# Attention and mixture of experts on one core: ScalarE copies the 16-bit planes, and a fifth expert's tokens are turned by DMA

## The chip, the core and the metric

The kernel runs as one program on one of the eight cores of a Trainium2 chip. The metric is the device time of one execution in microseconds (us); lower is better. Five engines work side by side, each on its own queue of instructions in a fixed order: TensorE (PE, matrix products), VectorE (DVE), ScalarE (ACT), GpSimd (POOL) and SyncE (SP, which here only issues DMA transfers). An instruction that waits holds up everything that stands behind it in its engine's queue.

## The reference, cut to what matters

```python
# attention: 8 batches, 8 heads, 576 positions, width 64, window of 128, a bias by distance
scores = scale * q @ k.T + bias;  attn = softmax(scores, masked);  x = (attn @ v)   # x: 4608 tokens x 512
# mixture of experts: 8 experts, each takes exactly cap = 4608 / 8 = 576 tokens
logits = x @ w_gate
for idx in argsort(-logits.flatten()):          # greedy: best pair first, until an expert is full
    ...
for e in range(8):
    h = maximum(x[assigned == e] @ w1[e], 0)    # 576x512 @ 512x1024
    out[assigned == e] = h @ w2[e]              # 576x1024 @ 1024x512
```

All of it is float32. Which tokens an expert gets is known only when the router has run, and an expert's list depends on which experts are already full.

## The kernel before, in words

**Attention** takes the first 230 us or so and is not touched. It leaves the tokens x in DRAM, one row of 512 floats for each token.

**The experts** follow one after another. "Expert k" below is the k-th in the order of processing, counted from 0, so the fourth expert is expert 3. Each float32 factor is split into a high and a low part (names ending in h and l), and a product is the sum of three matmuls. Layer 1 of an expert (`layer1`, L1041) runs over 8 blocks f of 128 hidden units; a block is 24 matmuls into two PSUM banks of a ring of four (`ph`). ScalarE then applies the ReLU into `hh` (L1064) and VectorE computes the low part `hlo` (L1069). Layer 2 (`layer2`, L1073) runs over five tiles t of tokens, 24 matmuls for each of the first four (L1087, L1088, L1090) and 16 for the last, into a ring of two banks (`po`); ScalarE copies a tile out (L1094) and GpSimd scatters it to DRAM (L1099). ScalarE and VectorE also split the weights, chunk by chunk (`split`, L965 and L967), after SyncE has loaded them (L958).

**The tokens of the next expert** are fetched by GpSimd with five indirect DMAs (`gather`, L976), one for each 128 tokens (the last has 64). A matmul needs them with features on the partitions, so each tile must be turned. There are two ways:

- `turn` (L987): PE transposes each tile in four pieces into one PSUM bank `pg` (L1000), ScalarE rounds it into `xh` (L1003), VectorE takes the rest into `xl` (L1004). All five tiles share that one bank. Experts 0 to 3 are turned in this way.
- `turn_by_dma` (L1008): the 32-bit words are taken apart into two planes of 16 bits (`pl`, two copies on GpSimd for each tile, L1017), SyncE issues a transposing DMA for each tile (`tp`, L1022), and two more copies on GpSimd join the planes to words again (`xf`, L1029). ScalarE and VectorE then make `xh` and `xl` (L1037, L1038). Experts 4 to 7 are turned in this way. All of `g`, `pl`, `tp` and `xf` live in one ring of seven buffers.

**The router** (`Router.phase`) runs in between, in small steps: for each next expert, several rounds of counting, each a VectorE indicator (L586), eight small matmuls (L610), a VectorE comparison and one more small matmul (L630); then sums (L760, L786, L787), the one-hot tables `loOH` and `mv` on VectorE (L812, L808, L809), 18 small matmuls that give the list (L817), and `idx` (L825). These small matmuls stand in PE's queue between those of the layers.

**What sets the order.** `layer_moe` calls `slot(k, i)` after each half block and each third of a tile, i counting from 0 to 30 within expert k. A slot advances the router when its count of slots to wait (table `WAITS`) has run out, loads and splits a chunk of weights, and takes the next step of the turning. `DMA_AT` holds, step by step, the slot from which a step of `turn_by_dma` may be taken: one step for the gathers, then five each for `pl`, `tp`, `xf` and `xh`/`xl`. `BY_DMA = 3` starts that way in the slots of expert 3, that is with the tokens of expert 4. The calls only give an order of creation; a scheduler then orders each engine's queue by its own estimates. A dependency marked `BEHIND` is seen by that scheduler alone and adds no wait on the chip; the transposes already have one ("weights first").

Of the kernel before, what the change touches and what calls it, by code (L numbers as in the profile page):

```python
# [423 lines left out]
TURN0 = 3  # L424
BY_DMA = 3
DMA_AT = [0, 1, 1, 2, 2, 2, 7, 7, 7, 7, 7, 9, 9, 10, 10, 10, 17, 19, 21, 23, 25]
BEHIND = mybir.DependencyInfo(mybir.DependencyClass.NoSync, mybir.DependencyReason.SCHED_ONLY)
# [32 lines left out]
class Router:  # L460
# [255 lines left out]
    def phase(self, k, exact=False):  # L716
# [94 lines left out]
        for a, z in ((0, 18), (18, 30), (30, NT)) if k == 0 else ((0, NT),):  # L811
            nc.vector.tensor_tensor(loOH[:, a:z], bc(self.C["i64"].rearrange("p (s o) -> p s o", o=2).unsqueeze(1), [128, z - a, 32, 2]),  # L812
                                    bc(slo[:, a:z].unsqueeze(2), [128, z - a, 32, 2]), ALU.is_equal)
        yield WAITS[6] + (k < 4)
        ip = self.bank()
# [13 lines left out]
        if k < 7:  # L829
            self.pen = self.small("pen", 8)  # L830
            nc.vector.tensor_scalar(self.pen, Dc, float(CAP), -BIG, ALU.is_ge, ALU.mult)
            self.base = self.small("base", 8)
            nc.vector.tensor_tensor(self.base, self.pen, Dc, ALU.add)
            nc.vector.scalar_tensor_tensor(self.left, keyv, mx[:, 0:1], self.left, ALU.not_equal, ALU.mult)
            L2 = rt.tile([128, 8, NT], F32, name="L2", bufs=1)
            eng = nc.vector if k == 0 or k > BY_DMA else self.tc.nc.gpsimd
            eng.tensor_tensor(L2, L, bc(self.pen.unsqueeze(2), [128, 8, NT]), ALU.add)
            if k == 0 or k > BY_DMA:
                nc.vector.scalar_tensor_tensor(self.L1, T1, 100.0 * BIG, L2, ALU.mult, ALU.add)
            else:  # L840
# [106 lines left out]
class MoE:  # L947
# [39 lines left out]
    def turn(self, gs, first=False):  # L987
# [6 lines left out]
        for h, (g, r) in enumerate(gs):  # L994
# [11 lines left out]
            yield  # L1006

    def turn_by_dma(self, idx, asked):  # L1008

# [3 lines left out]
        for g, r in gs:  # L1013
            pl = ring.tile([128, 2, DM], U16, name="pl", tag="g")
            words = g.bitcast(U16).rearrange("q (c o) -> q c o", o=2)
            for a in range(2):
                nc.gpsimd.tensor_copy(pl[:r, a, :], words[:r, :, 1 - a])  # L1017
            pls.append((pl, r))
            yield
        for pl, r in pls:  # L1020
# [3 lines left out]
            yield  # L1024
        for tp, r in tps:
            xf = ring.tile([128, 4, 128], F32, name="xf", tag="g")
            words = xf.rearrange("q j t -> q (j t)").bitcast(U16).rearrange("q (j t o) -> q j t o", j=4, o=2)
            for a in range(2):
                nc.gpsimd.tensor_copy(words[:, :, :r, 1 - a], tp[:, 4 * a:4 * a + 4, :r])  # L1029
            xfs.append((xf, r))  # L1030
            yield
        xh = self.p["xg"].tile([128, 4, CAP], F32R, name="xh")
        xl = self.p["xg"].tile([128, 4, CAP], F32R, name="xl")
        self.xg = xh, xl
        for h, (xf, r) in enumerate(xfs):
            o = slice(128 * h, 128 * h + r)
# [4 lines left out]
    def layer1(self, w1, xg, first=False):  # L1041
# [7 lines left out]
        for f, ts in order:  # L1049
# [12 lines left out]
            for t in ts:  # L1062
                o = hh[:, f, cut[t]:cut[t + 1]]
                nc.scalar.activation(o, pp[t], AF.Relu)  # L1064
                e = min(512, cut[t + 1])
# [7 lines left out]
    def layer2(self, w2, h, idx, last=False):  # L1073
        nc = self.nc
        hh, hl = h
        for t in range(5) if not last else (4, 0, 1, 2, 3):
# [4 lines left out]
            for cs in cols:  # L1081
# [11 lines left out]
                if t < 4:  # L1093
                    nc.scalar.copy(o[:, cs], po[:, cs])  # L1094
                else:
# [55 lines left out]
def layer_moe(tc, P, C, r, x, w1, w2, out, exact):  # L1151
# [29 lines left out]
    def slot(k, i):  # L1181
# [23 lines left out]
        if k >= BY_DMA and k + 1 in r.idx:  # L1205
            if k not in gathers:
                asked[k + 1] = []
                gathers[k], st["made"] = m.turn_by_dma(r.idx[k + 1], asked[k + 1]), 0
            while st["made"] < len(DMA_AT) and i >= DMA_AT[st["made"]]:
                next(gathers[k])  # L1210
                st["made"] += 1
# [106 lines left out]
```

## Time and profile before

| | |
|---|---|
| median of three runs | 692.59 us (692.06 to 695.39) |
| the profiled execution | 690.85 us, span of its instructions 688.9 us |
| expert 2, layer 1 and layer 2 | 356.64 to 385.30, 385.30 to 415.99 us of the span |
| expert 3 | 415.99 to 443.80, 443.80 to 471.17 |
| expert 4 | 471.17 to 498.25, 498.25 to 526.54 |
| expert 5 | 526.54 to 553.11, 553.11 to 579.48 |
| expert 6 | 579.48 to 605.06, 605.06 to 630.47 |

Each stage begins with the first matmul of its layer on PE's timeline. All times inside the span are counted from its start. In a list of waits, the engine, line and tile that waited stand left of the arrow, and what ended the wait on its right.

### The profile page before, as it was taken

Reading aid. Unit: us, or ns where it says so; the run is one execution under the profiler, and the core shown is the slowest. Engines: PE = TensorE matmul, PEld = TensorE weight load, DVE = VectorE, ACT = ScalarE, POOL = GpSimd, SP = SyncE. Lnnn points to the kernel's source line nnn. Section 1 sums busy time; section 2 is a strip of 40 time slices with the busy share of each in tenths; the row PEclk is TensorE's granted clock in tenths of the full one; section 3 lists DMA queues with packets and bytes.
Section 4 is the critical chain, followed back from the end, with each engine's and each line's share of the span. In section 5 each row is a group of like instructions: output and inputs, shape, how many; then the busy total and the mean of one; then the engine's idle time right before and its main releaser. Section 6 shows DMA issues by size and latency. Waiting matters only on the chain.

```text
span 688.9 us, 18916 instructions
## 1 busy us (share of the span) xinstructions
PE 657.4 (95%) x7171; PEld 582.2 (85%) x7172; DVE 479.1 (70%) x1985; ACT 332.1 (48%) x991; POOL 192.7 (28%) x376
## 2 busy tenths in 40 slices
PE   7999999999995699999999999999989999999995
PEld 4898998998985399889789779979978978988985
DVE  5788888888887899879669788886775734532310
ACT  6898888888884262334134224324323333432210
POOL 4021221211220301511422017255076075152011
PEclk9999999999997799999999999999999999999998
DMA  8456566566532453615417227635625644621001
GB/s 307 148 181 202 175 193 200 166 211 186 161 106 70 124 191 104 241 39 187 158 36 245 88 92 245 131 106 182 133 98 166 167 111 169 160 52 54 1 25 49
DMA packets 54212, 97.47 MB, mean 141 GB/s; under 512 B 22880, under 2 KB 32224, under 8 KB 54112
## 3 DMA queue, kind: packets, MB, share of 16 engines
q1 hardware_dynamic: 48224, 77.30, 37.0%
q0 software_dynamic: 5888, 18.88, 8.3%
q8 instruction: 58, 0.95, 0.6%
q14 instruction: 42, 0.34, 0.1%
HBM read 72.57 MB, written 18.87 MB: 133 GB/s over the span
## 4 chain that ended last, share of the span: by engine, by line
PE 77%; DVE 12%; DMA 6%; issue 2%; ACT 1%; SPq 1%; POOL 0%; POOLq 0%; DVEq 0%; ACTq 0%
PE ph L1059 20%; PE po L1087 9%; PE po L1088 9%; PE s L54 8%; PE pt L54 7%; PE pt L158 7%; PE po L1090 7%; PE x L54 6%; DMA raw<-in_w_dram 2%; DVE hl L967 2%; DMA tp<-pl 1%; DVE hlo L1069 1%; DMA craw<-in_cst_dram 1%; PE pg L1000 1%; DMA qk<-in_qk_dram 1%
## 5 line engine op out<-in xcount | busy, mean ns | idle before, releaser
L1059 PE MATMUL ph<-xh,hl 128*128 128x288 f32 (+2 forms) x1024 | 188.9, 299 | 0.7 <-DVE lo L534 0.5
L1059 PEld LDWEIGHTS ph<-xh,hl 128*128 128x128 f32 x1024 | 154.7, 189 | 2.4 <-ACT hh L1064 1.0
L145 ACT ACTIVATE u<-u,mn 128x192 f32<-128x192 f32 (+2 forms) x288 | 123.9, 433 | 24.6 <-DVE mn L134 24.5
L1087 PE MATMUL po<-hl,hh 128*128 128x512 f32 (+1 forms) x328 | 128.9, 393 | 0.6 <-ACT o L1094 0.6
L1088 PE MATMUL po<-hl,hh 128*128 128x512 f32 (+1 forms) x328 | 126.4, 385 | 0.0
L967 DVE TENSOR_TENSOR hl<-raw,hl 128x512 fp32r<-128x512 f32 x128 | 88.1, 708 | 48.6 <-ACT hl L965 48.1
L1059 PE MATMUL ph<-xl,hl 128*128 128x288 f32 (+2 forms) x512 | 115.1, 297 | 0.0
L1064 ACT ACTIVATE hh<-ph 128x288 fp32r<-128x288 f32 (+2 forms) x128 | 46.6, 408 | 131.9 <-PE ph L1059 128.8
L134 DVE CUSTOM_DVE_ANT_0 u<-s,bm 128x192 f32<-128x192 f32 x308 | 86.5, 333 | 29.8 <-PE s L54 29.2
L1090 PE MATMUL po<-hl,hlo 128*128 128x512 f32 (+1 forms) x264 | 101.3, 384 | 0.0
L1099 POOL DMA_INDIRECT out_dram<-o,idx x40 | 42.5, 1063 | 153.1 <-ACT o L1094 76.0
L1059 PEld LDWEIGHTS ph<-xl,hl 128*128 128x128 f32 x512 | 84.1, 189 | 0.0
L965 ACT CAST hl<-raw 128x1024 fp32r<-128x1024 f32 x64 | 65.8, 1050 | 25.1 <-DMA raw<-in_w_dram 22.0
L1069 DVE SCALAR_TENSOR_TENSOR hlo<-ph,hh 128x288 fp32r<-128x288 f32 (+2 forms) x128 | 49.4, 417 | 35.8 <-ACT hh L1064 35.1
L1087 PEld LDWEIGHTS po<-hl,hh 128*128 128x128 f32 x328 | 61.8, 188 | 12.3 <-ACT o L1094 1.0
L54 PE MATMUL s<-qk 64*64 64x192 f32 (+1 forms) x1112 | 69.6, 319 | 2.5 <-DVE mn L134 1.8
L1088 PEld LDWEIGHTS po<-hl,hh 128*128 128x128 f32 x328 | 61.8, 188 | 11.0
L1094 ACT COPY o<-po 128x512 f32<-128x512 f32 (+1 forms) x33 | 18.8, 572 | 95.7 <-PE po L1090 77.4
L976 POOL DMA_INDIRECT g<-x,idx x40 | 42.1, 1053 | 72.2 <-issue 31.7
L1090 PEld LDWEIGHTS po<-hl,hlo 128*128 128x128 f32 x264 | 49.6, 188 | 10.0
L158 PE MATMUL pt<-ident_sb,u 128*128 128x128 f32 x368 | 54.2, 282 | 1.4 <-DVE mn L134 1.0
L54 PEld LDWEIGHTS s<-qk 64*64 64x64 f32 x1112 | 48.3, 132 | 8.3 <-issue 2.2
(240 smaller groups left out, 925.8 us busy)
## 6 DMA issues: line engine op xcount, KB each, us to landing
raw<-in_w_dram SPq DMA_DIRECT2D x64, 512.0 KB, 4.4
qk<-in_qk_dram SPq DMA_DIRECT2D x32, 576.0 KB, 4.8
v<-in_v_dram SPq DMA_DIRECT2D x32, 288.0 KB, 3.8
x<-xb SPq DMA_DIRECT2D x14, 512.0 KB, 3.5
x<-xb SPq DMA_DIRECT2D x8, 128.0 KB, 3.3
x<-xb SPq DMA_DIRECT2D x4, 256.0 KB, 2.4
g<-x,idx POOLq DMA_INDIRECT x40, 3.9
out_dram<-o,idx POOLq DMA_INDIRECT x40, 3.2
```

Source lines behind the costliest of these rows:

```text
L54: put(nc.tensor.matmul(out, w, a, start=start, stop=stop, skip_group_check=True))
L134: put(nc.vector.tensor_tensor_reduce(out=u[rows], in0=x[rows, c:c + 64 * m].rearrange("q (j k) -> q j k", k=64), in1=bm[n % NP][rows, y:y ...
L145: put(nc.scalar.activation(u, u, AF.Exp, bias=st["mn"][:, i:i + 1], scale=-1.0, accum_out=st["sm"][:, i:i + 1]))
L158: put(nc.tensor.transpose(ps[:, c:c + 128], u[:, o + 128 * j:o + 128 * j + 128], ident))
L965: self.last = nc.scalar.copy(hl[:, 0, :], raw)
L967: nc.vector.tensor_tensor(hl[:, 1, c:c + 512], raw[:, c:c + 512], hl[:, 0, c:c + 512].bitcast(F32), ALU.subtract)
L1059: nc.tensor.matmul(pp[t], w[:, a, j, fo:fo + 128], x[:, j, cut[t]:cut[t + 1]], start=(i == 0), stop=(i == 11))
L1064: nc.scalar.activation(o, pp[t], AF.Relu)
L1069: nc.vector.scalar_tensor_tensor(d, pp[t][:, c0:c1], 0.0, o[:, c0:c1].bitcast(F32), ALU.max, ALU.subtract)
L1087: nc.tensor.matmul(out, a, wh, start=(f == 0), stop=False)
L1088: nc.tensor.matmul(out, a, wl, start=False, stop=(f == 7 and t == 4))
L1090: nc.tensor.matmul(out, hl[:, f, 128 * t:128 * t + 128], wh, start=False, stop=(f == 7))
```

## The change

Four edits go together.

1. The four plane copies of each tile in `turn_by_dma` move from GpSimd to ScalarE (`nc.scalar.copy`), and each is ordered by the scheduler behind the last ReLU or output copy that ScalarE was given before it (`behind`).
2. Joining a tile and splitting it into `xh` and `xl` become one step instead of two.
3. `BY_DMA` becomes 2: the tokens of expert 3 are turned by DMA as well, and expert 3's PE transposes go.
4. `DMA_AT` becomes a table for expert 2's slots and one for all later ones, and the list of every expert from 4 on is made one slot later (`WAITS[6] + 1` for all).

```diff
-BY_DMA = 3
-DMA_AT = [0, 1, 1, 2, 2, 2, 7, 7, 7, 7, 7, 9, 9, 10, 10, 10, 17, 19, 21, 23, 25]
+BY_DMA = 2
+DMA_AT = {2: [10, 11, 11, 12, 12, 12, 13, 13, 13, 13, 13, 23, 24, 25, 26, 27], 3: [0, 4, 5, 6, 7, 8, 9, 9, 9, 9, 9, 18, 20, 22, 24, 26]}
...
-        yield WAITS[6] + (k < 4)
+        yield WAITS[6] + 1
...
-            eng = nc.vector if k == 0 or k > BY_DMA else self.tc.nc.gpsimd
+            eng = nc.vector if k == 0 or k > 3 else self.tc.nc.gpsimd
...
+    def behind(self, copy):
+        self.tc.add_manual_dep(copy.ins, self.acted.ins.name, BEHIND, reason="layers first")
+
     def turn_by_dma(self, idx, asked):
...
-                nc.gpsimd.tensor_copy(pl[:r, a, :], words[:r, :, 1 - a])
+                self.behind(nc.scalar.copy(pl[:r, a, :], words[:r, :, 1 - a]))
...
-        for tp, r in tps:
+        xh = self.p["xg"].tile([128, 4, CAP], F32R, name="xh")
+        xl = self.p["xg"].tile([128, 4, CAP], F32R, name="xl")
+        self.xg = xh, xl
+        for h, (tp, r) in enumerate(tps):
             xf = ring.tile([128, 4, 128], F32, name="xf", tag="g")
             words = xf.rearrange("q j t -> q (j t)").bitcast(U16).rearrange("q (j t o) -> q j t o", j=4, o=2)
             for a in range(2):
-                nc.gpsimd.tensor_copy(words[:, :, :r, 1 - a], tp[:, 4 * a:4 * a + 4, :r])
-            xfs.append((xf, r))
-            yield
...
-        for h, (xf, r) in enumerate(xfs):
+                self.behind(nc.scalar.copy(words[:, :, :r, 1 - a], tp[:, 4 * a:4 * a + 4, :r]))
...
-                nc.scalar.activation(o, pp[t], AF.Relu)
+                self.acted = nc.scalar.activation(o, pp[t], AF.Relu)
...
-                    nc.scalar.copy(o[:, cs], po[:, cs])
+                    self.acted = nc.scalar.copy(o[:, cs], po[:, cs])
...
-            while st["made"] < len(DMA_AT) and i >= DMA_AT[st["made"]]:
+            due = DMA_AT[min(k, 3)]
+            while st["made"] < len(due) and i >= due[st["made"]]:
```

In the changed kernel the copies of `pl` stand on L1020, the transposes on L1025 and the copies of `xf` on L1035.

How the instructions move is seen at three places. The first is ScalarE's queue in layer 1 of expert 2, from its third and fourth block on (a row with x4 is two blocks of the ReLU). Before:

```order
L1064 ACTIVATE hh<-ph 128x288 x4
L965 CAST hl<-raw 128x1024
L1064 ACTIVATE hh<-ph 128x288 x4
L965 CAST hl<-raw 128x1024
L1064 ACTIVATE hh<-ph 128x288 x4
L965 CAST hl<-raw 128x1024
L1094 COPY o<-po 128x512
L1003 CAST xh<-pg 128x4x128
```

and now:

```order
L1064 ACTIVATE hh<-ph 128x288 x4
L965 CAST hl<-raw 128x1024
L1064 ACTIVATE hh<-ph 128x288 x4
L1020 COPY pl<-g 128x512 x8
L1020 COPY pl<-g 64x512 x2
L1064 ACTIVATE hh<-ph 128x288 x2
L965 CAST hl<-raw 128x1024
L1064 ACTIVATE hh<-ph 128x288 x2
L965 CAST hl<-raw 128x1024
L1094 COPY o<-po 128x512 x2
L1035 COPY xf<-tp 128x512 x2
L1037 CAST xh<-xf 128x4x128
```

All ten `pl` copies of expert 3's tokens stand in one block between the ReLU of block 5 and that of block 6, and a chunk of weights is split after them.

The second place is ScalarE's queue at the end of layer 1 and in layer 2 of expert 3 (the tokens are those of expert 4). Before:

```order
L1064 ACTIVATE hh<-ph 128x288 x4
L1037 CAST xh<-xf 128x4x128 x4
L1037 CAST xh<-xf 128x4x64
L965 CAST hl<-raw 128x1024
L1094 COPY o<-po 128x512 x4
L965 CAST hl<-raw 128x1024 x4
```

and now:

```order
L1064 ACTIVATE hh<-ph 128x288 x4
L965 CAST hl<-raw 128x1024
L1094 COPY o<-po 128x512
L1035 COPY xf<-tp 128x512 x3
L1037 CAST xh<-xf 128x4x128
L1035 COPY xf<-tp 128x512
L1037 CAST xh<-xf 128x4x128
L1094 COPY o<-po 128x512
L1035 COPY xf<-tp 128x512 x2
L1037 CAST xh<-xf 128x4x128
L1094 COPY o<-po 128x512
```

The five `xh` stood ahead of the first output copy; now they follow it, with their `xf` copies, spread between the output copies. The slots of experts 4, 5 and 6 read the same.

The third place is VectorE's queue in layer 2 of expert 4, where the list of expert 6 is made (`hif` to `mv`) and the tokens of expert 5 are split (`xl`). Before:

```order
L1038 TENSOR_TENSOR xl<-xf,xh 128x4x128
L847 SCALAR_TENSOR_TENSOR ov<-kmx,ov 128x1
L792 TENSOR_SCALAR hif<-m 128x36
L848 TENSOR_TENSOR flag<-flag,ov 128x1
L500 TENSOR_TENSOR ne<-L_72,b 128x288
L793 TENSOR_SCALAR hif<-hif 128x36
L1038 TENSOR_TENSOR xl<-xf,xh 128x4x128
L795 SCALAR_TENSOR_TENSOR hv<-hif,m 128x72
L800 SCALAR_TENSOR_TENSOR slo<-hif,m 128x72
L797 TENSOR_TENSOR hOH<-c_h_431,hv 128x360
L812 TENSOR_TENSOR loOH<-c_i_429,slo 128x2304
L808 TENSOR_TENSOR mv<-hOH,c_cc 128x36x10
```

and now:

```order
L795 SCALAR_TENSOR_TENSOR hv<-hif,m 128x72
L800 SCALAR_TENSOR_TENSOR slo<-hif,m 128x72
L797 TENSOR_TENSOR hOH<-c_h_431,hv 128x360
L812 TENSOR_TENSOR loOH<-c_i_429,slo 128x2304
L808 TENSOR_TENSOR mv<-hOH,c_cc 128x36x10
L809 TENSOR_SCALAR mv<-hOH,craw 128x36x10
L504 TENSOR_REDUCE am<-cand 128x36
L505 TENSOR_TENSOR OH<-c_eb,am 128x288
L757 TENSOR_TENSOR T_8654<-OH,sel 128x288
L1038 TENSOR_TENSOR xl<-xf,xh 128x4x128 x2
```

Two `xl` stood ahead of `mv`; now all stand behind it, and two halves of a weight split (L967) stand ahead of it instead, above the rows shown. On PE, the 18 matmuls of that list (L817) stand behind 42 matmuls of layer 2 instead of 33, in the layers of experts 3 and 4 alike.

More of the change, by code (lines that the diff above doesn't have):

```diff
@@ L835, in phase @@
             L2 = rt.tile([128, 8, NT], F32, name="L2", bufs=1)
-            eng = nc.vector if k == 0 or k > BY_DMA else self.tc.nc.gpsimd
+            eng = nc.vector if k == 0 or k > 3 else self.tc.nc.gpsimd
             eng.tensor_tensor(L2, L, bc(self.pen.unsqueeze(2), [128, 8, NT]), ALU.add)
-            if k == 0 or k > BY_DMA:
+            if k == 0 or k > 3:
                 nc.vector.scalar_tensor_tensor(self.L1, T1, 100.0 * BIG, L2, ALU.mult, ALU.add)
@@ L1028, in turn_by_dma @@
             for a in range(2):
-                nc.gpsimd.tensor_copy(words[:, :, :r, 1 - a], tp[:, 4 * a:4 * a + 4, :r])
-            xfs.append((xf, r))
-            yield
-        xh = self.p["xg"].tile([128, 4, CAP], F32R, name="xh")
-        xl = self.p["xg"].tile([128, 4, CAP], F32R, name="xl")
-        self.xg = xh, xl
-        for h, (xf, r) in enumerate(xfs):
+                self.behind(nc.scalar.copy(words[:, :, :r, 1 - a], tp[:, 4 * a:4 * a + 4, :r]))
             o = slice(128 * h, 128 * h + r)
```

## The prediction

> **What bounds the kernel now.** First the engines of the page, then the busy times by stage, from layer 1 of expert 2 to layer 2 of expert 6 (columns: start and end, length, busy time and count of PE, its weight loads, VectorE, ScalarE and GpSimd, granted clock, DMA share, GB/s).
>
> ```profile
> PE 657.4 (95%) x7171; PEld 582.2 (85%) x7172; DVE 479.1 (70%) x1985; ACT 332.1 (48%) x991; POOL 192.7 (28%) x376
> ...
> 356.64:385.30 28.66, 27.25 (x223) 26.50 (x221) 27.01 (x108) 9.80 (x19) 7.48 (x8) 1.00 0.58 194
> 385.30:415.99 30.69, 30.11 (x173) 23.27 (x172) 23.42 (x102) 9.04 (x15) 5.57 (x5) 1.00 0.20 67
> 443.80:471.17 27.37, 26.28 (x134) 21.44 (x133) 20.81 (x69) 9.20 (x15) 19.42 (x26) 1.00 0.31 102
> 498.25:526.54 28.29, 26.34 (x134) 21.45 (x133) 15.13 (x34) 9.31 (x15) 22.51 (x28) 1.00 0.33 104
> 553.11:579.48 26.37, 25.75 (x115) 20.94 (x113) 7.33 (x13) 9.22 (x15) 20.75 (x27) 1.00 0.35 115
> 579.48:605.06 25.58, 25.58 (x193) 25.58 (x192) 14.85 (x35) 9.18 (x19) 2.82 (x3) 1.00 0.71 190
> 605.06:630.47 25.41, 25.41 (x114) 21.03 (x113) 7.43 (x13) 8.80 (x14) 12.05 (x14) 1.00 0.15 48
> ```
>
> PE is the bound: in expert 6 it is busy without a gap, 25.58 us for a layer 1 and 25.41 us for the 112 matmuls of a layer 2, so 25.41/112 = 0.227 us from one to the next. The clock is 1.00 everywhere. Time can only be won where a stage is longer than these two: in layer 2 by 5.28 us for expert 2 and by 1.96, 2.88 and 0.96 us for experts 3, 4 and 5. GpSimd, on the other hand, is busy there for some 20 us without setting anything by itself. Who makes PE wait in experts 3 to 5, from the list of waits of PE between 415.99 and 580 us (total, times, longest):
>
> ```profile
> PE m L817 <- DVE mv L809: 3.0, 2, 1.9
> PE po L1087 <- ACT o L1094: 0.6, 1, 0.6
> ```
>
> Two waits for the router's table `mv` and one for an output copy; the rest of the excess is the router's own small matmuls. What makes `mv` and the copy late stands in the timelines of VectorE and ScalarE (start, length, instruction, idle time before it and what ended it):
>
> ```profile
> 446.19 1.07 DVE L1038 TENSOR_TENSOR xl<-xf,xh 128x512 fp32r<-128x512 f32 x1
> ...
> 452.36 0.30 DVE L809 TENSOR_SCALAR mv<-hOH,craw 128x360 bf16<-128x360 bf16 x1
> ...
> 500.85 0.69 DVE L1038 TENSOR_TENSOR xl<-xf,xh 128x512 fp32r<-128x512 f32 x1 [0.86 <-ACT xh L1037]
> ...
> 507.71 0.30 DVE L809 TENSOR_SCALAR mv<-hOH,craw 128x360 bf16<-128x360 bf16 x1
> ...
> 562.91 0.41 ACT L1037 CAST xh<-xf 128x256 fp32r<-128x256 f32 x1 [1.09 <-POOL xf L1029]
> 563.22 1.04 ACT L965 CAST hl<-raw 128x1024 fp32r<-128x1024 f32 x1
> 564.16 1.06 ACT L1094 COPY o<-po 128x512 f32<-128x512 f32 x2
> ```
>
> All three come from the turned tokens: VectorE takes an `xl` before `mv` and waits with it for ScalarE's `xh`; ScalarE waits for GpSimd's last `xf` until 562.9 us and only then comes to the output copies.
>
> **The change, part by part.** *Expert 3's transposes go.* PE's timeline in layer 2 of expert 2 shows them between the matmuls of the layer; here the second, the fourth and the fifth tile:
>
> ```profile
> 397.74 0.39 PE L1090 MATMUL po<-hl,hlo 128*128 128x512 f32 x1
> 397.97 0.60 PE L1000 MATMUL pg<-ident_sb,g 128*128 128x128 f32 x4
> 398.32 0.48 PE L1087 MATMUL po<-hl,hh 128*128 128x512 f32 x1
> ...
> 406.26 0.39 PE L1090 MATMUL po<-hl,hlo 128*128 128x512 f32 x1
> 407.23 0.66 PE L1000 MATMUL pg<-ident_sb,g 128*128 128x128 f32 x4 [0.58 <-DVE xl L1004]
> 407.64 0.47 PE L1087 MATMUL po<-hl,hh 128*128 128x512 f32 x1
> ...
> 411.51 0.40 PE L1090 MATMUL po<-hl,hlo 128*128 128x512 f32 x1
> 411.84 0.46 PE L1000 MATMUL pg<-ident_sb,g 64*128 64x64 f32 x4
> 412.23 0.50 PE L1087 MATMUL po<-hl,hh 128*128 128x512 f32 x1
> ```
>
> From one layer matmul to the next there are 0.58, 1.38 and 0.72 us where 0.227 would do: 0.35, 1.15 (with a wait for the one bank) and 0.49. With three tiles like the first: 3 x 0.35 + 1.15 + 0.49 = **2.7 us**.
>
> *The waits of experts 3 to 5.* By the order in VectorE's queue, no `xl` stands before `mv` any more, and L817 stands nine matmuls later on PE (9 x 0.227 = 2.0 us), which alone covers the longest wait of 1.9. The output copy of a first tile stands ahead of all `xf` and `xh`. So 3.0 + 0.6 = **3.6 us** go. What is late next is `xl` of the last tile, needed when the next layer 1 begins: in experts 3 to 5 ScalarE has some 3 us of copies left after its third output copy, and 5.5 us of PE work (24 x 0.227) until the fourth.
>
> *What a plane copy costs on ScalarE.* No row has ScalarE on 16-bit words. The nearest:
>
> ```profile
> L1017 POOL COPY pl<-g x40: 600/607/1062, 421.1 to 575.3; 128x512 uint16<-128x512 uint16 x32, 64x512 uint16<-64x512 uint16 x8
> L1029 POOL COPY xf<-tp x40: 464/770/1562, 442.7 to 613.2; 128x512 uint16<-128x512 uint16 x32, 128x256 uint16<-128x256 uint16 x8
> L1037 ACT CAST xh<-xf x20: 404/620/625, 444.5 to 613.7; 128x512 fp32r<-128x512 f32 x16, 128x256 fp32r<-128x256 f32 x4
> L1038 DVE TENSOR_TENSOR xl<-xf,xh x20: 408/687/1165, 446.2 to 614.2; 128x512 fp32r<-128x512 f32 x16, 128x256 fp32r<-128x256 f32 x4
> L965 ACT CAST hl<-raw x64: 1040/1050/1060, 233.3 to 628.9; 128x1024 fp32r<-128x1024 f32 x64
> ```
>
> The rows give minimum, median and maximum in ns. ScalarE takes 620 ns for 512 elements and 1050 for 1024, so it goes by elements; below stands 404 ns (256 elements), above GpSimd's 1562 for the same copy. I take 0.6 us, being nearest to ScalarE's own 512 elements; then 20 copies are 12 us for an expert, on an engine busy for 18 of 51 us. The Trainium skill, ScalarE: Activation LUTs, What ACT_TABLE_LOAD costs, gives 186 ns plus 0.833 ns for each element whatever the type, an estimate of 0.61 us; the two ScalarE medians agree with it, and the sum by it would be the same.
>
> *The block of ten in expert 2.* It stands behind the ReLU of block 5. ScalarE's timeline and GpSimd's gathers of that list (first and last of five, then the time to landing):
>
> ```profile
> 377.67 0.71 ACT L1064 ACTIVATE hh<-ph 128x288 fp32r<-128x288 f32 x2 [3.16 <-PE ph L1059]
> ...
> 380.87 0.71 ACT L1064 ACTIVATE hh<-ph 128x288 fp32r<-128x288 f32 x2 [1.55 <-PE ph L1059]
> 385.37 0.71 ACT L1064 ACTIVATE hh<-ph 128x288 fp32r<-128x288 f32 x2 [3.79 <-PE ph L1059]
> ...
> 372.20 1.00 POOL L976 DMA_INDIRECT g<-x,idx  x1 [10.99 <-issue]
> 377.51 0.91 POOL L976 DMA_INDIRECT g<-x,idx  x1 [0.30 <-issue]
> ...
> DMA to landing us min/median/max: 2.9/3.9/7.8
> ```
>
> The first tile is there at 377 us, the last at about 382.3. Ten copies from 378.4 end at 384.4, so the ReLU of block 6 comes at 384.4 instead of 380.9, that of block 7, behind a weight split of 1.05, at 386.1. PE does not need them at once: block 7 uses the banks that block 5 left, and layer 2 comes to f = 6 only 18 matmuls (4.1 us) after 385. But VectorE waits with `hlo`, and the router's counting stands behind it; PE reaches L630 and the third L610 there at 387 and 391 us, and VectorE would be ready some 0.3 and 0.4 us later. Against this, the first L610 stood 0.7 us still for work that now comes later. I charge **0.5 us**, between -0.7 and 2.5.
>
> *Transposing DMAs.* Five more go onto SyncE. Those of expert 4, with the weight loads around them:
>
> ```profile
> 433.05 0.33 SPq L958 DMA_DIRECT2D raw<-in_w_dram  x1
> 433.55 9.52 SPq L1022 DMA_TRANSPOSE tp<-pl  x5
> 444.54 33.36 SPq L958 DMA_DIRECT2D raw<-in_w_dram  x6
> ```
>
> They hold SyncE for 9.5 us. In expert 2 they stand behind a load issued at 378.4 us and ahead of one that waits until 399 us for the next list's expert, so they fit from 380 to 390 and land before ScalarE asks for them after its second output copy, at about 397. Nothing else queues on SyncE meanwhile. From 397 ScalarE works through ten `xf` and five `xh` (9 us) and two output copies until about 410.3, `xl` of the last tile ends near 411, and layer 1 of expert 3 would begin at about 412: just in time, and free.
>
> *GpSimd gives up its copies.* They held nothing on the path but `xf`, counted above. In the row of `xl` an instruction of 687 ns takes up to 1165 ns, the long ones while GpSimd copies (1.07 at 446.19). The Trainium skill, SBUF: State Buffer, Who interferes with whom, says that GpSimd and a VectorE instruction with two SBUF inputs exclude each other and that ScalarE has ports of its own. The trace agrees as far as these rows go; by that rule `mv` also comes sooner, which makes the 3.6 us surer but not larger.
>
> The sum: 2.7 + 3.6 - 0.5 = **5.8 us**. The profiled execution took 690.85 us (span 688.9), 1.7 below the median of the runs; I take the 5.8 off the median: 692.6 - 5.8 = **686.8 us**.
>
> **The rivals.** *A, the waits move.* ScalarE becomes the engine for which VectorE waits, and the router's small matmuls stand still again, only elsewhere. For it: in layer 1 of experts 3 to 6 ScalarE's queue has four copies behind the ReLU of block 2, four more and a weight split behind that of block 3, and a block lasts only 25.58/8 = 3.2 us; a late ReLU makes VectorE's `hlo` late, and in experts 3 and 4 a comparison for L630 stands behind it. Against it: ReLU and four copies, 0.8 + 4 x 0.6 = 3.2 us, are no longer than a block. If only the transposes are won, or only the waits: 2.7 to 3.6, 689 to 690 us.
>
> *B, slower: 16-bit copies are dear on ScalarE.* For it: no row excludes it; on GpSimd the strided write of `xf` takes 770 ns against 607. Against it: ScalarE's rows go by elements. At 1.05 us a copy (as long as 1024 elements of `hl`), the block in expert 2 ends at 388.9 and holds L630 for some 4 us. In layer 1 of experts 3 to 6 the ReLU of block 3 is 0.8 + 4.2 - 3.2 = 1.8 us late, that of block 4 is 1.8 + 0.7 + 4.2 + 1.05 - 3.2 = 4.55 us late, and its banks are wanted one block later: 4.55 + 0.7 - 3.2 = 2 us of standing still, four times, 8. The last `xl` of expert 3 is 1.7 us late. 13.7 lost against 6.3 won: 692.6 + 7.4 = 700 us. At 0.85 the same steps give 2 + 4 x 0.45 + 2 x 0.75 (L630) + 0.5, about 6, so it decides from 0.87 us a copy.
>
> *C, the change doesn't reach the waits.* If a transposing DMA lands after ScalarE has come to its `xf`, ScalarE's whole queue stands, output copies among it, where so far only GpSimd's stood. It would have to land 7 us later than worked out in expert 2 and 4 us later in the others; then gain and loss cancel, near 692.6 us.
>
> **How the numbers follow.** The forecast 0.70, A 0.16, B 0.10, C 0.04. Half a per cent of 692.6 is 3.5 us, about what a measurement of this kernel can tell from no change: below 689.1 is faster. Of A a quarter lies there, so faster 0.70 + 0.04 = 0.74; the rest of A, a fifth of B and half of C make the same, 0.16; slower 0.10. The low end is the forecast without the charge and with the 0.7 us (685.6), less 1.6 for the runs' scatter: 684.0. The high end, 691.5, takes in A with its scatter; B and the end of C are left out. The forecast's own range is 685 to 689.
>
> **What would show it.** Right: no L1000 in expert 2 and its layer 2 near 27.5 us; layer 2 of experts 3 to 5 near 26.3, 26.3 and 25.7; no wait of L817 for `mv`; plane copies near 0.6 us. Wrong: waits of PE for `sat`, `ind` or `hh` in layer 1 of experts 2 to 4 (A); copies above 0.87 us (B); ScalarE's `xf` waiting for `tp` (C).

## The result and the profile after

| | before | changed | ratio (95%) |
|---|---|---|---|
| median of the runs | 692.54 us | 682.94 us (681.70 to 686.24) | 0.986 (0.9815 to 0.9906) |
| the profiled execution | 690.85 us | 683.86 us | |
| its span | 688.9 us | 681.7 us | |

The changed kernel is faster, by 9.6 us between the medians and by 7.0 between the profiled executions. The time is 1.1 us below the low end of the predicted range. The engines of the changed kernel's page, and the same stages as in the prediction, from layer 1 of expert 2 to layer 2 of expert 5 (the columns are those of the prediction: start and end, length, busy time and count of PE, its weight loads, VectorE, ScalarE and GpSimd, granted clock, DMA share, GB/s):

```profile
PE 655.0 (96%) x7152; PEld 580.3 (85%) x7152; DVE 468.5 (69%) x1985; ACT 386.4 (57%) x1091; POOL 134.2 (20%) x296
...
356.28:385.71 29.43, 27.73 (x230) 26.68 (x229) 27.06 (x108) 14.47 (x29) 7.47 (x8) 1.00 0.59 194
385.71:412.75 27.04, 27.04 (x145) 21.38 (x144) 21.91 (x99) 14.54 (x25) 4.96 (x5) 1.00 0.43 117
412.75:440.42 27.67, 27.61 (x221) 26.72 (x220) 22.89 (x81) 14.99 (x30) 6.20 (x6) 1.00 0.68 188
440.42:466.59 26.17, 26.17 (x135) 21.38 (x134) 17.64 (x68) 15.04 (x25) 8.16 (x9) 1.00 0.44 129
466.59:493.67 27.08, 27.08 (x221) 26.56 (x220) 20.94 (x77) 14.29 (x29) 1.69 (x2) 1.00 0.68 167
493.67:519.87 26.20, 26.20 (x135) 21.37 (x134) 12.79 (x35) 15.04 (x25) 8.13 (x9) 1.00 0.43 125
519.87:546.27 26.40, 26.40 (x215) 26.18 (x213) 19.07 (x59) 14.35 (x29) 2.09 (x2) 1.00 0.64 182
546.27:571.68 25.41, 25.41 (x115) 21.03 (x113) 6.80 (x13) 15.05 (x25) 8.13 (x9) 1.00 0.49 118
```

ScalarE has taken 54 us of work, GpSimd has lost 58, and PE is busy without a gap in every layer 2 of experts 2 to 5. The list of waits of PE between 356 and 640 us no longer names L817 or an output copy; what is left lies in layer 1 of expert 2:

```profile
PE m L610 <- DVE ind L586: 0.9, 1, 0.9
PE ph L1059 <- ACT hh L1064: 0.5, 1, 0.5
PE m L787 <- DVE run L780: 0.3, 1, 0.3
```

Stage by stage against before: layer 2 of expert 2 is shorter by 3.65 us (30.69 to 27.04), its layer 1 longer by 0.77 (28.66 to 29.43); layer 2 of experts 3, 4 and 5 is shorter by 1.20, 2.09 and 0.96, layer 1 of experts 3 and 5 by 0.14 and 0.17. Together 7.4 us. The other stages up to layer 1 of expert 7 agree within 0.01 us; what lies ahead of expert 2 is 0.4 us shorter, and the end, from layer 2 of expert 7 on, 0.6 us longer.

The plane copies on ScalarE (minimum, median and maximum in ns):

```profile
L1020 ACT COPY pl<-g x50: 613/623/633, 378.0 to 586.7; 128x512 uint16<-128x512 uint16 x40, 64x512 uint16<-64x512 uint16 x10
...
L1035 ACT COPY xf<-tp x50: 482/772/787, 398.1 to 616.4; 128x512 uint16<-128x512 uint16 x40, 128x256 uint16<-128x256 uint16 x10
```

Taking the planes apart costs what was assumed, 0.62 us; joining them, with a strided write, costs 0.77.

### The profile page after: what moved, and what is told of

Read it like the earlier page. It is cut to its first block, busy times and chain, and to the rows that moved or that the text cites. A ratio compares the mean times of both kernels' runs of the same rounds, so it can differ in the third digit from the quotient of the medians.

```text
span 681.7 us, 18901 instructions
## 1 busy us (share of the span) xinstructions
PE 655.0 (96%) x7152; PEld 580.3 (85%) x7152; DVE 468.5 (69%) x1985; ACT 386.4 (57%) x1091; POOL 134.2 (20%) x296
## 4 chain that ended last, share of the span: by engine, by line
PE 86%; DVE 8%; DMA 3%; issue 1%; ACT 1%; POOL 0%; SPq 0%; POOLq 0%; DVEq 0%; ACTq 0%
PE ph L1059 24%; PE po L1087 10%; PE po L1088 10%; PE s L54 9%; PE po L1090 8%; PE pt L54 7%; PE pt L158 7%; PE x L54 6%; DMA raw<-in_w_dram 2%; DVE hl L967 2%; DVE hlo L1069 1%; PE m L610 1%; DVE u L134 1%; PE pg L1000 1%; PE ph L984 1%
## 5 line engine op out<-in xcount | busy, mean ns | idle before, releaser
L967 DVE TENSOR_TENSOR hl<-raw,hl 128x512 fp32r<-128x512 f32 x128 | 85.1, 684 | 22.0 <-ACT hl L965 21.6
L145 ACT ACTIVATION_READ_ACCUMULATOR u<-u,mn 128x1 f32 x288 | 54.4, 189 | 0.0
```

Of the source, the lines that this page charges most:

```text
L145: put(nc.scalar.activation(u, u, AF.Exp, bias=st["mn"][:, i:i + 1], scale=-1.0, accum_out=st["sm"][:, i:i + 1]))
L967: nc.vector.tensor_tensor(hl[:, 1, c:c + 512], raw[:, c:c + 512], hl[:, 0, c:c + 512].bitcast(F32), ALU.subtract)
```

## The experiments

### The changed kernel and the kernel before in further sets of runs

No edit; each set stands beside its own runs of the kernel before.

> The changed kernel itself, in more rounds. Stage by stage, the two profiled executions differ by 7.2 us, the medians of four runs by 9.6. If the terms are all there is, the ratio is 0.989 to 0.991 (6.3 to 7.5 us of 692). If something beside the stages became shorter that one profiled execution does not show, the ratio stays at 0.986 (9.6 us).

> The changed kernel once more, beside the next three on one chip. Between the first runs and the second the ratio went from 0.986 to 0.992, with two new things in the profile: the ReLU of block 5 in expert 2 began 2 us after its matmuls, and PE's granted clock halved for 3.4 us after a wait of 1.35 us. Theory: neither belongs to the kernel; where the ReLU comes in time, the ratio is 0.985 to 0.988; where it comes 2 us late, 0.990 to 0.994. Rival: the first four runs were only lucky; then 0.992 whatever the ReLU does.

> The changed kernel for the third time, as a base for the next three. Ratio 0.991 if the ReLU of block 5 in expert 2 begins 2 us late again, 0.986 if it doesn't.

> The kernel before, profiled on the same chip as the changed one. Theory: ratio 1.000; if this chip delays the ReLU of block 5 in expert 2 by 2 us, before is delayed too (its layer 1 of expert 2 at 30 us instead of 28.7), and the difference by stages to the changed kernel is 2.9 us in layer 2 of expert 2 and 4 us in experts 3 to 5, whatever the chip.

| set | before | changed | ratio (95%) |
|---|---|---|---|
| first | 692.54 | 682.94 | 0.986 (0.9815 to 0.9906) |
| e1_after | 693.93 | 688.55 | 0.9918 (0.9889 to 0.9947) |
| e5_after_2 | 693.57 | 687.77 | 0.9916 (0.9889 to 0.9943) |
| e12_after_3 | 692.69 | 686.41 | 0.9924 (0.9900 to 0.9949) |

(us; e6_before_2, the kernel before under a name of its own, had 692.90 us and ratio 0.9991.) The gain is 5.4 to 6.3 us in the three further sets, not 9.6. Before stayed within 1.4 us in these four (in the set of e9_dear, e10_third and e11_engine it had 695.16 us), so it is the changed kernel that was 3.5 to 5.6 us faster in the first set. In e1_after the gain of 5.4 us lies below the 6.3 to 7.5 us that the stages let expect, though the interval takes in the expected ratio of 0.989 to 0.991. The ratios of e5_after_2 and e12_after_3 are near those that were expected with a late ReLU; but in no further set of the changed kernel was the ReLU in time, so the rival, that the first four runs were lucky, is not excluded.

The profiles show a part of it. Between the first profile of the changed kernel and that of e12_after_3, layer 1 of expert 2 grows from 29.43 to 30.40 us, layer 1 of expert 3 from 27.67 to 28.99, and three more stages by 0.3 to 0.4: 3.4 us in all. (The two executions differ by 1.8 us alone, since the end, from layer 2 of expert 7 on, is 1.5 us shorter.) ScalarE's timeline at block 5 of expert 2, in the first profile of the changed kernel and then in e1_after:

```profile
373.53 0.71 ACT L1064 ACTIVATE hh<-ph 128x288 fp32r<-128x288 f32 x2 [1.67 <-PE ph L1059]
377.39 0.71 ACT L1064 ACTIVATE hh<-ph 128x288 fp32r<-128x288 f32 x2 [3.15 <-PE ph L1059]
377.99 3.22 ACT L1020 COPY pl<-g 128x512 uint16<-128x512 uint16 x6
```

```profile
373.70 0.71 ACT L1064 ACTIVATE hh<-ph 128x288 fp32r<-128x288 f32 x2 [1.88 <-PE ph L1059]
379.47 0.71 ACT L1064 ACTIVATE hh<-ph 128x288 fp32r<-128x288 f32 x2 [5.06 <-remote]
380.07 5.29 ACT L1020 COPY pl<-g 128x512 uint16<-128x512 uint16 x10
```

The ReLU of block 4 begins at the same time, that of block 5 two us later, and the trace names no instruction of this core that releases it ("remote"). A second such start follows near 423 us, in layer 1 of expert 3. VectorE's `hlo` and the counting behind it are late by as much, and PE waits for them, here in e12_after_3:

```profile
PE m L630 <- DVE sat L627: 1.4, 1, 1.4
PE m L610 <- DVE ind L586: 1.3, 1, 1.3
```

The kernel before has the first late start as well where it was profiled again (e6_before_2: layer 1 of experts 2 and 3 is 29.63 and 28.68 us, 1.0 and 0.9 longer than in its first profile). Its median is only 0.4 us higher there than in the first set, which speaks against the late starts being the whole of the fall from 9.6 us; the rest stays open.

**A wait of PE can cost more than itself.** PE's granted clock around the wait for L610 in e1_after (start and end, length, busy time and count, clock, DMA share, GB/s):

```profile
381.00:382.00 1.00, 0.43 (x2) 1.00 0.94 299
382.00:383.00 1.00, 0.07 (x3) 1.00 0.53 176
383.00:384.00 1.00, 1.00 (x13) 0.79 0.00 0
384.00:385.00 1.00, 1.00 (x6) 0.50 0.00 0
...
386.00:387.00 1.00, 1.00 (x6) 0.50 1.05 196
387.00:388.00 1.00, 1.00 (x15) 1.00 0.94 184
```

Behind a wait of 1.36 us the clock is halved from 383.6 to 387.0, 3.4 us, which costs another 1.7: layer 1 of expert 2 lasts 31.97 us here, and 30.40 in e12_after_3, where a wait of 1.34 us leaves the clock at 1.00. Whether it happens depends on when the wait comes. The halved stretches and those at the end of the attention part lie a multiple of 3.41 us apart in every profile. The wait of L817 in expert 4 shows it on the kernel before, in its first profile and in e6_before_2, cut along that grid:

```profile
503.57:506.98 3.41, 2.55 (x12) 1.00 0.00 0
506.98:510.39 3.41, 2.33 (x26) 1.00 0.00 0
510.39:513.80 3.41, 3.41 (x16) 1.00 0.22 82
```

```profile
503.90:507.31 3.41, 3.41 (x16) 1.00 0.01 4
507.31:510.72 3.41, 1.38 (x23) 1.00 0.00 0
510.72:514.13 3.41, 3.41 (x13) 0.50 0.00 0
```

A wait of 1.94 us spread over two windows left the clock alone; one of 2.02 inside a single window halved it in the next, and layer 2 of expert 4 took 29.99 us instead of 28.29. The Trainium skill, TensorE: Matmul & The Clock Gate, What's actually happening, describes a window of 3413 ns that runs freely and sets the clock to half or full by how busy PE was in it; the length and the grid agree with these rows. The rule of the Trainium skill, TensorE: Matmul & The Clock Gate, HAM oscillation — how this bites in real kernels, that no gap of PE be longer than some 3.4 us, does not agree: 1.36 us were enough here.

### Expert 3's tokens by PE again

```diff
-BY_DMA = 2
+BY_DMA = 3
```

> The changed kernel, but expert 3's tokens are turned on PE again, as before the change; experts 4 to 7 keep their copies on ScalarE. By the prediction's terms 2.7 us of transposes come back and the 0.5 us charge of expert 2's layer 1 goes: 2.2 us over the changed kernel; by the stages of the two traces 3.65 - 0.77 = 2.9 us, layer 2 of expert 2 at 30.7 us and its layer 1 at 28.7. Rival: the five transposes only fill time in which PE would wait for something else; then it is within 1 us of the changed kernel.

688.68 us, beside 688.55 for the changed kernel on the same chip (means -0.4, plus or minus 1.7): no difference clear of the scatter, and the 2.2 us that were expected lie outside it. The stages move as the term said, layer 2 of expert 2 is 30.55 us against 27.06. But layer 1 of expert 2 takes 30.18 against 31.97 and layer 1 of expert 3 28.53 against 29.00. So with the late start the 3.5 us of the transposes are for the most part given back (1.8 + 0.5), 1.7 of it by the halved clock of that one profile. Between the two first profiles, without the late start, 2.9 of the 3.65 were kept; no run had the transposes back without the late start, so this rests on those two profiles alone.

### The block of ten, spread out

```diff
-DMA_AT = {2: [10, 11, 11, 12, 12, 12, 13, 13, 13, 13, 13, 23, 24, ...
+DMA_AT = {2: [10, 12, 13, 14, 15, 16, 16, 16, 16, 16, 16, 23, 24, ...
```

> The changed kernel, but in expert 2 the ten plane copies pl don't stand in one block behind the ReLU of block 5: each pair stands behind one of blocks 6 and 7 or a later step, the transposing DMAs follow one step after the last. By the theory that the block of ten is what costs expert 2's layer 1 its 0.8 us (2.5 to 3.3 with a halved clock), this layer 1 goes back to 28.7 us and the time falls by 0.8 to 3 us against the changed kernel. Rival: the copies only move the standing still into layer 2, because the transposing DMAs land later: layer 1 of expert 3 begins late by 1 us or more, no gain or a loss.

688.18 us against 687.77 (means -0.5, plus or minus 2.1): no difference clear of the scatter. The ReLU of block 6 now begins at 382.65 us (385.26 in e1_after), and still L610 waits for 1.36 us, as it does in e2_pe_turns (1.27), where no plane copy stands in this layer at all. The wait comes from the late ReLU of block 5, not from the block of ten behind it. What the block itself costs is another matter: layer 1 of expert 2 is 31.32 us here, of which a halved clock (384.60 to 388.01 us) makes 1.7; without it this is 29.6, against 30.3 to 30.9 in e1_after, e12_after_3 and e5_after_2. Layer 2 of expert 2 gives 0.4 of that back (27.44 us).

### L817 alone, and all but L817

On the kernel before (e4), and on the changed kernel (e7):

```diff
-        yield WAITS[6] + (k < 4)
+        yield WAITS[6] + 1
```

```diff
-        yield WAITS[6] + 1
+        yield WAITS[6] + (k < 4)
```

> The kernel before, with one edit of the change alone: L817 of experts 4 and later stands one slot later on PE. By the prediction nine matmuls (2.0 us) cover the longest of its waits (1.9 us) by themselves: 3.0 us less than before (ratio 0.9957), layer 2 of experts 3, 4, 5 some 0.8, 1.6, 0.6 us shorter. Rival: VectorE is late by GpSimd's copies and the standing still only moves to the next thing that PE wants of VectorE or ScalarE: within 1 us of before.

> The changed kernel, but L817 of experts 4 and later stands one slot earlier, as in the kernel before. The prediction gave two reasons for the end of L817's waits, VectorE's order and the later place. If VectorE's order (no xl ahead of mv, no copies on GpSimd) is enough, nothing changes: within 1 us of the changed kernel, no wait of L817 for mv. If the later place did it, L817 waits again, 1 to 2 us in each of experts 3 to 5: 2 to 4 us over the changed kernel.

The later L817 alone makes the kernel before slower: 696.51 us, ratio 1.0035 (1.0014 to 1.0056). L817 waits 0.6 us in all where it waited 3.0, and two new waits take the place of the rest: 2.1 us for `hlo` and 1.5 for `ei`. VectorE's timeline shows what is behind the first, GpSimd's what runs meanwhile:

```profile
473.28 3.63 DVE L967 TENSOR_TENSOR hl<-raw,hl 128x512 fp32r<-128x512 f32 x1
```

```profile
473.54 2.82 POOL L1017 COPY pl<-g 128x512 uint16<-128x512 uint16 x5
```

An instruction whose median is 0.68 us lasts until GpSimd's plane copies are through. With the later list the gathers and these copies come later too: in before nine of the ten were through at 470.9 us, here the last five run until 476.4, where VectorE needs the second part of the weights and then `hlo`.

Without the later L817 the changed kernel takes 689.50 us against 687.77 (means +1.5, plus or minus 2.4). L817 does not wait, layer 2 of experts 3 to 5 is 26.17, 26.20 and 25.41 us as in the changed kernel; what is longer lies in layer 1 of experts 2 (31.74 against 30.85, a halved clock) and 3 (29.76 against 28.91). So what changed on VectorE's side ends the waits of L817; the later place isn't needed for it, and alone it only moves them. On VectorE's side two things changed, no copies on GpSimd beside it and no `xl` ahead of `mv`. In e7_old_wait, and in e11_engine below, both hold, so the runs don't separate them.

### The copies on GpSimd, with the new steps

```diff
-                self.behind(nc.scalar.copy(pl[:r, a, :], words[:r, :, 1 - a]))
+                nc.gpsimd.tensor_copy(pl[:r, a, :], words[:r, :, 1 - a])
...
-                self.behind(nc.scalar.copy(words[:, :, :r, 1 - a], tp[:, 4 * a:4 * a + 4, :r]))
+                nc.gpsimd.tensor_copy(words[:, :, :r, 1 - a], tp[:, 4 * a:4 * a + 4, :r])
```

> The changed kernel, but the plane copies (pl and xf) stand on GpSimd, with the same steps, the same transposing DMAs for expert 3 and L817 one slot later. By the prediction, xh then waits on ScalarE for GpSimd's xf and holds the output copy behind it, and VectorE's xl comes late again: layer 2 of experts 2 to 5 loses 0.5 to 1 us each, 2 to 4 us over the changed kernel; the charge of expert 2's layer 1 (0.8 us) goes. Rival: ScalarE was not needed, the later L817 and the transposing DMAs alone give the gain: within 1 us of the changed kernel.

703.77 us, ratio 1.0116 (1.0077 to 1.0154): 15 us over the changed kernel, several times what was expected, and 10 over before. Of VectorE's and GpSimd's timelines in expert 2, and of PE's waits:

```profile
378.48 0.29 DVE L860 TENSOR_SCALAR q<-b,hi,half 128x36 f32<-128x36 f32 x1
...
379.29 3.70 DVE L861 TENSOR_SCALAR q<-q,half,rw 128x36 f32<-128x36 f32 x1
379.56 3.39 POOL L1020 COPY pl<-g 128x512 uint16<-128x512 uint16 x6
```

```profile
PE m L610 <- DVE ind L586: 5.3, 2, 4.5
PE ph L1059 <- DVE hlo L1069: 4.3, 2, 2.3
PE m L786 <- DVE ei L773: 2.7, 1, 2.7
```

An instruction on 36 elements, 0.30 us otherwise, stands for 3.70 us while GpSimd copies. Four halved stretches of PE's clock follow these waits. The Trainium skill, SBUF — State Buffer, Who interferes with whom, has VectorE and GpSimd share a port pair that one locks against the other; the rows agree. In these rows GpSimd's copies do not only make VectorE's instructions somewhat longer, they stop it for whole trains of copies. ScalarE is what makes the new steps possible.

### The engine alone, with the old steps

The kernel before with its plane copies on ScalarE, `behind` included, but `BY_DMA`, `DMA_AT` and L817 as they were:

```diff
-                nc.gpsimd.tensor_copy(pl[:r, a, :], words[:r, :, 1 - a])
+                self.behind(nc.scalar.copy(pl[:r, a, :], words[:r, :, 1 - a]))
...
-                nc.gpsimd.tensor_copy(words[:, :, :r, 1 - a], tp[:, 4 * a:4 * a + 4, :r])
+                self.behind(nc.scalar.copy(words[:, :, :r, 1 - a], tp[:, 4 * a:4 * a + 4, :r]))
```

> The kernel before, with the engine of the plane copies changed alone: on ScalarE, behind its last ReLU or output copy, with the old steps (ten pl behind the first ReLU of layer 1, ten xf behind the second last), expert 3's tokens on PE and L817 as before. If what VectorE loses to GpSimd's copies is the cause of the waits of experts 3 to 5, L817 no longer waits and layer 2 of experts 3 to 5 is 26.2, 26.2 and 25.4 us: 4 us less. If the steps matter as much, the ten copies in a row (5.5 to 7 us) hold the ReLUs of block 1 and block 7 and PE waits for hh or for a bank: layer 1 of experts 3 to 6 is 1 to 3 us longer each and the kernel no faster than before.

703.41 us, ratio 1.0137 (1.0109 to 1.0166). L817 no longer waits, but layer 2 now does; PE's longest group of waits, and ScalarE's timeline at the end of layer 1 of expert 3:

```profile
PE po L1087 <- ACT hh L1064: 8.3, 4, 3.0
```

```profile
445.90 6.04 ACT L1029 COPY xf<-tp 128x512 uint16<-128x512 uint16 x10 [1.97 <-issue]
451.82 0.68 ACT L1064 ACTIVATE hh<-ph 128x288 fp32r<-128x288 f32 x2
```

Ten `xf` in a row hold the last ReLU of layer 1 back by 5 to 7 us in each of four experts, and two of these waits halve the clock. Engine and steps are both needed: either alone is 8 to 10 us slower than before (in e3_gpsimd the steps come with expert 3's transposing DMAs and the later L817; the later L817 cost 2.6 us by itself in e4_before_l817).

### Dearer copies on ScalarE

```diff
-                self.behind(nc.scalar.copy(pl[:r, a, :], words[:r, :, 1 - a]))
+                for c in (256, DM):
+                    self.behind(nc.scalar.copy(pl[:r, a, :c], words[:r, :c, 1 - a]))
...
-                self.behind(nc.scalar.copy(words[:, :, :r, 1 - a], tp[:, 4 * a:4 * a + 4, :r]))
+                for c in (2, 4):
+                    self.behind(nc.scalar.copy(words[:, :c, :r, 1 - a], tp[:, 4 * a:4 * a + c, :r]))
```

> The changed kernel, with each plane copy on ScalarE preceded by a copy of its first half, so that a pl costs about 1.03 us and an xf about 1.2 us, above the 0.87 us from which rival B decides. By rival B's steps (4 us in expert 2, 2 us of standing still in layer 1 of each of experts 3 to 6, 1.7 us before layer 1 of expert 3) the time rises by some 13 us over the changed kernel, more where a wait halves PE's clock. Against it: the steps DMA_AT spread the copies and PE looks two blocks ahead; then 0 to 4 us.

683.60 us, ratio 0.986 (0.9818 to 0.9901): 0.7 us above the changed kernel's first set and below its three others, where some 13 us more were expected. The changed kernel was not run on the same chip. ScalarE's timeline in layer 1 of expert 4:

```profile
477.27 0.71 ACT L1066 ACTIVATE hh<-ph 128x288 fp32r<-128x288 f32 x2 [0.36 <-PE ph L1061]
477.86 3.40 ACT L1021 COPY pl<-g 128x256 uint16<-128x256 uint16 x8
481.16 0.72 ACT L1066 ACTIVATE hh<-ph 128x288 fp32r<-128x288 f32 x2
481.76 3.40 ACT L1021 COPY pl<-g 128x256 uint16<-128x256 uint16 x8
485.06 0.71 ACT L1066 ACTIVATE hh<-ph 128x288 fp32r<-128x288 f32 x2
```

A train of eight takes 3.40 us, so a plane copy with its extra half occupies ScalarE for 0.85 us and not for the sum of the single durations, 1.03; in the changed kernel four take 2.18 and each occupies 0.55. At 0.85 rival B's steps came to a loss of some 6 us. The ReLUs of blocks 3 and 4 are indeed late, by 0.7 and 0.9 us against the changed kernel when both are counted from the start of the layer, and PE waits for neither: layer 1 of expert 4 takes 26.96 us. In the changed kernel a weight split stands ahead of the ReLU of block 4, here behind it, so the order isn't quite the one that rival B priced. In layer 1 of expert 3 PE waits 0.7 us for the last `xh` (rival B: 1.7).

### Another place in ScalarE's stream

Ahead of the attention, on the changed kernel (e13) and on the kernel before (e15):

```diff
+    pad = P["c"].tile([1, 1], F32, name="pad")
+    nc.vector.memset(pad, 0.0)
+    for i in range(32):
+        nc.scalar.copy(pad, pad)
```

> The changed kernel with 32 copies of one element on ScalarE ahead of the attention, while it waits for its first data: every later instruction of ScalarE stands 32 places further, nothing else moves. If the late ReLU hangs on the place in ScalarE's stream (its instructions arrive late there), the stall moves to another instruction, one with slack perhaps, and the time changes by 2 us or more in either direction against e12_after_3. If it hangs on the data or on PE, the ReLU of block 5 is late again and the time is within 1 us.

> The kernel before with the same 32 copies. If the stall hangs on the place in the stream, the ReLU of block 5 in expert 2 is in time here too and layer 1 of expert 2 takes 28.7 us instead of 29.6; the kernel gains at most 1.5 us by it, since it lost only 1.0 + 0.9 in layer 1 of experts 2 and 3. If not, within 1 us of before with the late ReLU.

689.09 us beside 686.41, and 695.29 beside 692.69. Both are 2.6 to 2.7 us longer, where at most 1 was expected. Expert 2 begins 2.5 us later than in e12_after_3 and 4.2 later than in e6_before_2, with PE's clock halved for 3.4 and 10.2 us near the start of the attention; e5_after_2 and e7_old_wait have such a stretch (6.8 us) without the copies, so how much the copies cost themselves is not separated. The stages of the experts agree within 0.7 us up to layer 1 of expert 7. The late start is again at block 5 of expert 2, in both (381.63 and 384.23 us). So 32 places more in ScalarE's stream do not move it. In e10_third, e14_third_2 and e11_engine the ReLU of block 5 came within 0.3 us of its time, in e9_dear 1.6 us late. What it waits for stays open.

### Expert 2's tokens by DMA as well

```diff
-BY_DMA = 2
-DMA_AT = {2: [10, 11, ...
+BY_DMA = 1
+DMA_AT = {1: [16, 18, 19, 20, 20, 21, 21, 21, 21, 21, 21, 25, 26, 27, 28, 29], 2: [10, 11, ...
```

> The changed kernel, and expert 2's tokens turned by DMA as well (BY_DMA 1, with steps 16 to 29 for that list, all in layer 2 of expert 1). Layer 2 of expert 1 held 30.4 us with PE's transposes; by what expert 2's layer 2 gave (30.6 to 27.05) it falls to about 27, 3.4 us. If ScalarE's last xh and VectorE's last xl come in time, the ratio falls by 0.005 against the changed kernel. Rival: the steps are too late, layer 1 of expert 2 waits for xl and gives back 2 us or more, and the router's work of expert 1 slips into a later wait.

> The version with expert 2's tokens by DMA, on the same chip as the changed kernel. By the stages of the profiles it is ahead by 1.4 in layer 2 of expert 1 and by 1.5 to 4 in layer 1 of expert 2, and loses 0.9 in layer 2 of expert 2: 2 to 4.5 us. Rival: all of its lead came from where the stall fell, and it is within 1 us of the faster of e12_after_3 and e13_shift.

681.89 us, ratio 0.9826 (0.9795 to 0.9858), and in the second set 682.77, ratio 0.9879 (0.9852 to 0.9907), 3.6 us less than the changed kernel on the same chip (means -3.1, plus or minus 2.3). The stages from layer 2 of expert 1 to layer 1 of expert 3, first in e12_after_3, then in e14_third_2:

```profile
325.91:356.71 30.80, 29.54 (x162) 23.24 (x161) 18.56 (x71) 8.83 (x14) 10.73 (x10) 1.00 0.32 111
356.71:387.11 30.40, 28.07 (x230) 26.85 (x229) 27.33 (x109) 14.78 (x29) 7.47 (x8) 1.00 0.59 190
387.11:414.15 27.04, 27.04 (x145) 21.38 (x144) 21.61 (x97) 14.22 (x25) 5.01 (x5) 1.00 0.42 114
414.15:443.14 28.99, 27.59 (x221) 26.69 (x220) 22.98 (x81) 15.00 (x30) 6.20 (x6) 1.00 0.65 177
```

```profile
325.28:354.33 29.05, 27.44 (x142) 21.30 (x141) 15.86 (x65) 16.57 (x30) 9.35 (x9) 1.00 0.55 155
354.33:382.22 27.89, 27.26 (x223) 26.49 (x221) 26.22 (x104) 16.55 (x32) 8.70 (x8) 1.00 0.60 200
382.22:410.11 27.89, 27.61 (x153) 21.53 (x152) 23.73 (x105) 15.40 (x27) 5.33 (x5) 1.00 0.46 118
410.11:438.51 28.40, 27.47 (x221) 26.59 (x220) 22.80 (x81) 14.98 (x30) 5.41 (x6) 1.00 0.66 186
```

Layer 2 of expert 1 gives 1.75 us (3.4 were expected): PE's busy time falls by 2.1, and a new wait of L630 for VectorE takes 0.7 back. (In the other sets of the changed kernel this stage has 30.4 us, 0.4 less than in e12_after_3.) Layer 1 of expert 2 gives 2.5; there the ReLU of block 5 is in time and L610 waits 0.3 instead of 1.34 us. Layer 2 of expert 2 loses 0.85. Its lead over e9_dear, 1.7 us on one chip, lies within the scatter (means -2.0, plus or minus 2.5). It has the lowest median of all versions here, and in e14_third_2 it is ahead of both kernels on one chip.

## Why the prediction was right or wrong

The direction was right, the time (686.8) too high for the measurement on record, and the low end of the range by 1.1 us. Of the 9.6 us, 7.0 lie between the two profiled executions (7.4 in the stages, where 5.8 were forecast); 1.7 come from before's profiled execution lying below its median and 0.9 from the changed kernel's lying above its own. In the later sets (686.4 to 688.6) the time lies inside the range, but this is in part luck: the stages won more than forecast, and late starts that nobody forecast took some of it back.

- *"3 x 0.35 + 1.15 + 0.49 = 2.7 us"* was mis-sized; this is the first step that failed. Layer 2 of expert 2 gave 3.65. Eight small matmuls (L610, 0.27 us) only moved into layer 1. The rest is 3.4, of which 0.5 is a thing I had not counted, the layer matmul behind each group of transposes. The timeline of before at the second tile:

```profile
398.32 0.48 PE L1087 MATMUL po<-hl,hh 128*128 128x512 f32 x1
398.64 0.39 PE L1088 MATMUL po<-hl,hh 128*128 128x512 f32 x1
```

  From the first to the second there are 0.32 us instead of 0.227; five times 0.09 is 0.5. The last 0.2 us I can't assign.
- *"3.0 + 0.6 = 3.6 us"*: layer 2 of experts 3 to 5 gave 4.25 and their layer 1 another 0.3; the forecasts of 26.3, 26.3 and 25.7 us were 26.17, 26.20 and 25.41. The waits went. But the reason *"L817 stands nine matmuls later on PE, which alone covers the longest wait"* was wrong: alone it makes the kernel slower (e4_before_l817), and without it the waits do not come back (e7_old_wait). The other reason, the order in VectorE's queue, stands, together with one that I had set aside, GpSimd's copies; the runs don't separate these two.
- *"GpSimd gives up its copies. They held nothing on the path but xf"* was wrong as a general statement. In before the old steps put most of the copies where VectorE had time; in the two other placings that were run (e3_gpsimd, e4_before_l817) they stop it for up to 3.7 us. For the sum of this change it made no difference, for what makes the change work it is the main point.
- *"I charge 0.5 us, between -0.7 and 2.5"*: 0.77, of which 0.27 are the moved L610. The size was about right and the ReLUs of blocks 6 and 7 came at 384.57 and 386.10 us, as worked out (384.4 and 386.1), but by luck: the copies took less than 0.6 us each, and a wait of 1.28 us for the gathered tokens, left out of the sum, made up for it. In the later sets this stage lost 1.0 to 2.5 us more, and e8_spread and e2_pe_turns show that the block of ten is not the cause of the wait for L610.
- *Plane copies at 0.6 us*: `pl` 0.62, `xf` 0.77; single durations. In a train each occupies ScalarE for less: four `pl` take 2.18 us and three `xf` 2.03, so 0.55 and 0.68 each. The 0.6 was near enough for the sum.
- *"I take the 5.8 off the median: 692.6 - 5.8"* is the second step that failed, with *"less 1.6 for the runs' scatter"*. The terms were worked out on an execution 1.7 us below its median, and the one of the changed kernel lay 0.9 above its own. I took the scatter of before's runs as the scatter of the difference; in truth the first set of the changed kernel and the later ones differ by 3.5 to 5.6 us. Small delays end in waits of PE and a wait may halve the clock, but that is not all: at the same mean granted clock, 0.985 or 0.986, runs took 681.70 to 683.86 us in the first set, 685.58 to 685.90 in e12_after_3 and 686.71 to 688.59 in e1_after. What else differs stays open.
- *Rival A, the waits move*, had the signs right that it named (PE waiting for `ind` and `sat` in layer 1 of experts 2 and 3), and in the later sets they are longer; the stages of e12_after_3 lost 3.4 us against the first profile. What starts them is the late ReLU, not the copies in ScalarE's queue, as far as e8_spread and e2_pe_turns show.
- *Rival B* fell by e9_dear: at 0.85 us a copy there is no loss, where its steps gave 6 us. At this price its steps make the ReLU of block 4 2.95 us late; in expert 4 it was 0.9 late, in part because the weight split (1.05 us) moved behind it, and that never reached PE. Copies at 1.05 us were not run. *Rival C*: no `xf` waits for its transposing DMA in the changed kernel, and the last `xh` of expert 3 ends at 411.0 us, in time for layer 1 at 412.75. `xl` of the last tile ended at 413.2 us and not near 411; PE's list of waits has nothing for it.

## What to carry to other kernels

Before trusting a gain of one per cent, run the same pair in several sets: here the same two kernels gave 9.6 and 5.4 us. When helper work moves to another engine, move its steps too, and spread them behind the instructions that the critical engine waits for: the engine alone and the steps alone were each 8 to 10 us slower than the old kernel. Price an inserted PE instruction to the second matmul behind it, and a wait of PE at up to 1.7 us more than its length.

## What the runs showed of the hardware that was not expected

- PE's granted clock goes by windows of 3.41 us. Among the experts every window with PE busy for 0.42 of it or less was followed by one at half the clock (e3_gpsimd, e6_before_2, e11_engine, e15_before_shift), and every window from 0.57 up by one at full clock. Between 0.47 and 0.56 both occur: 0.48 (e4_before_l817), 0.55 (e8_spread) and 0.56 (e1_after, e7_old_wait) halved it; 0.47 (e7_old_wait), 0.49 and 0.52 (e11_engine) and 0.54 (e4_before_l817) did not. Waits of 1.36 to 2.0 us can suffice if they fall into one window.
- GpSimd's strided 16-bit copies stop VectorE for whole trains: 3.63 us for a 0.68 us subtraction (e4_before_l817), 3.70 for an instruction on 36 elements (e3_gpsimd).
- ScalarE's strided 16-bit write costs 0.77 us for 512 elements where the strided read costs 0.62 (the changed kernel).
- ScalarE began one ReLU 1.4 to 2.0 us late in twelve of the fifteen later profiles and not in the first two, with no releaser in the trace. 32 places more in ScalarE's stream did not move it (e13_shift); the cause is open.
